# Sliding-window attention, Mish layer and experts: the activation, the weight conversion, the normalisation and the order of the blocks are rewritten

## The chip, the cores and the metric

One core of a Trainium2 chip runs the whole program. The metric is the device time of one execution in microseconds (us); the median of several executions is given. TensorE (PE, with its weight loads as PEld), VectorE (DVE), ScalarE (ACT), GpSimd (POOL) and SyncE (SP, here the issuer of DMAs) have queues of their own, each worked off in order.

## What is computed

```python
# q, k, v: (2, 8, 768, 64); window 128, 4 sinks
scores = matmul(q, k.T) / sqrt(64)
keep = (pos < n_sink) | ((rel >= 0) & (rel < window))
a = softmax(where(keep, scores, -1e9))            # sum + 1e-9
x = matmul(a, v)                                  # -> 1536 tokens x 512
h = x @ w_in                                      # 512 -> 2048, float64 weights
x = (h * tanh(softplus(h))) @ w_out               # 2048 -> 512, float64 weights
p = probs / (probs.sum(-1) + 1e-9)
out = sum(p[:, e] * (relu(x @ w1[e]) @ w2[e]) for e in range(4))   # 512 -> 1024 -> 512
```

## The kernel before, in words

**Attention.** `banded` goes over 24 items (batch, block of 256 queries, pair of heads). `attention_item` makes four score tiles of 128 queries each (two heads `j`, two halves `t`), in PSUM bank `sc`. VectorE adds the mask and takes the maximum (line 273), ScalarE the exponential with its sum (277), VectorE adds 1e-9 and takes the reciprocal (278, 279). Then the probabilities `pr` are normalised in place (286, 289): `c.turn("norm")` deals the two heads of items 0 to 15 to VectorE and GpSimd in turn, and those of items 16 to 23 to GpSimd alone. TensorE transposes them (309), ScalarE copies the result (311), TensorE multiplies with `v` (323), and `evac_x` writes the attention output as a high and a low part, `xh` (204) and `xl` (205). Blocks after the first one have four sink columns; three small VectorE copies (298 to 300) gather them as high, high and low parts, two transposes (316) and one matmul with `vsk` (328) add them.

The first `FP_ITEMS` = 16 items multiply float32 scores directly (two matmul records a tile). The last eight split `qk` into `hi` and `lo` (`attention_prep`, 239) and use three single-pass matmuls a tile.

**The first layer pair.** The hidden dimension of 2048 is cut into units 0 to 3 of 512. Each unit's float64 weights come as pairs of 32-bit words and are converted in pieces of [128, 512] by `split_double` (line 136 on ScalarE, 137 to 139 and 141 to 144 on VectorE): four operations with one tensor input, three with two. The high part goes to its tile by a DMA from `cv_h`. A unit has eight such pieces. `layer1` makes blocks `h` of 128 hidden features x up to 512 tokens with 12 matmuls, `mish` turns each into `gh` and `gl`, and `layer2` makes blocks `o` of 12 matmuls from four of these. `mish` is four ScalarE operations (571 to 574), two VectorE operations (575, 576), a square on ScalarE (578), another VectorE operation (579), and a product, a rounded copy and a difference, which from unit 1 on are all GpSimd's (583, 111, 121). For unit 0 the `Turns` lists mix the engines.

**The second layer pair.** Units 4 to 11 are the four experts in halves; ReLU on ScalarE (508), the low part on VectorE (509), the weighted sum on VectorE (558); GpSimd splits the float32 weights (111, 121).

**Order.** `stream` yields all four `h` of a chunk of tokens, then all four `o` of the chunk before. Unit 0's stream is interleaved with the attention: `banded` draws one step after each item from item `LAG` = 12 on, and two conversion pieces after each item. This sets priorities: a scheduler at compile time fixes the order of each queue, and moves later steps ahead where it expects an engine to be free. During the attention there is one PSUM bank for `h` and one for `o`; later there are four of each. `gh` and `gl` have six buffers each.

Of the kernel before, what the change touches and what calls it, by code (L numbers as in the profile page):

```python
# [18 lines left out]
C2, C1, C0 = 0.4889076793633006, -0.9463237919407588, -0.8989585617169157  # L19
TINY_HI = 3.4332275390625e-05  # L20
# [6 lines left out]
LAG = 12  # L27
FP_ITEMS = 16
WARM = 12


ENGINES = dict(
    norm=16 * "vp" + 16 * "p", sq="a", sq0=8 * "v" + 8 * "a", g="p", g0="pv", gh="p", gh0="ap", gl="p",
    gl0=8 * "p" + 8 * "v",
)


class Turns:


    def __init__(self, nc, **lists):
        engines = {"a": nc.scalar, "v": nc.vector, "p": nc.gpsimd}
        self.lists = {k: [engines[x] for x in v] for k, v in lists.items()}
        self.n = dict.fromkeys(lists, 0)

    def __call__(self, kind):
        self.n[kind] += 1
        return self.lists[kind][(self.n[kind] - 1) % len(self.lists[kind])]

# [35 lines left out]
def setup(c):  # L85
# [4 lines left out]
    ident_r = c.const.tile([P, P], F32R, name="ident_r")  # L90
    nc.vector.tensor_copy(ident_r, ident)
    c.ident_r = ident_r
    zero = c.acc[:, 2, 0:P]
    nc.gpsimd.memset(zero, 0.0)
    c.zero = zero
# [28 lines left out]
def split_double(c, pool, hi, lo, words):  # L124
# [7 lines left out]
    a = pool.tile([P, n], I32, tag="cv_a", name="cv_a")  # L132
# [23 lines left out]
def sink_values(c, a):  # L156

    nc = c.nc
    n = c.B * c.H // 2
    raw = c.acc[0:96, 4:6].rearrange("p a w -> p (a w)").rearrange("p (n d) -> p n d", n=n)  # L160
    nc.gpsimd.memset(raw, 0.0)
    for r in range(3):
        nc.sync.dma_start(out=raw[32 * r:32 * r + 2 * SINKS], in_=c.vsink)
    vsk = a.one.tile([96, n, P], F32R, name="vsk")
    nc.gpsimd.tensor_scalar(vsk, raw, 1.0, 0.0, ALU.mult, ALU.add)
    nc.gpsimd.tensor_tensor(vsk[32:64], raw[32:64], vsk[32:64].bitcast(F32), ALU.subtract)
    return vsk


def mask_parts(c):  # L170
# [11 lines left out]
    c.masks = [c.const.tile([P, P + SEG], F32, name=f"mask{i}") for i in range(3)]  # L182
# [25 lines left out]
def attention_pools(c, ctx):  # L208
    nc = c.nc
    a = Ctx()  # L210
    a.one = ctx.enter_context(c.tc.tile_pool(name="a_one", bufs=1))
# [4 lines left out]
    a.st = ctx.enter_context(c.tc.tile_pool(name="a_st", bufs=1))  # L216
# [5 lines left out]
    for t in a.sk:  # L222
        nc.vector.tensor_copy(
            t.rearrange("p n s d -> p n (s d)"), c.zero[:, 0:96].unsqueeze(1).to_broadcast([P, 2, 96])
        )
# [538 lines left out]
```

## Time and profile before

| | |
|---|---|
| median of 3 runs | 973.71 us (973.03 to 981.35) |
| the profiled execution, its own time | 972.71 us |
| its span, first to last instruction | 970.9 us |
| TensorE busy, records | 930.2 us (96%), 4292 |
| VectorE busy | 507.2 us (52%) |
| ScalarE busy | 330.6 us (34%) |
| GpSimd busy | 334.9 us (34%) |
| mean granted TensorE clock | 0.968 of full speed |

Matmuls are pipelined, so the durations of TensorE's records overlap and its busy time says little; how far apart matmuls start, and how many records fall into a stretch, says more. Shares over the whole span mix stages with different limits, so the rows further down are taken by stage.

### The profile page before, as it was taken

The numbers are of one execution on the slowest core, as the hardware profiler recorded it, in microseconds if no ns is written. First come the engines' busy times: TensorE is split into PE (matmuls) and PEld (weight loads), VectorE is DVE, ScalarE is ACT, GpSimd is POOL, SyncE is SP. The second block draws the span as 40 slices with busy tenths as digits, with TensorE's granted clock in tenths as the row PEclk, the third lists the DMA queues.
The fourth block names the chain that finished last, engine by engine and source line by source line (L and its number), as shares of the span: only waits on it lengthen the run. The fifth ranks groups of instructions, "written<-read, shape, count | busy, mean of one in ns | idle before, by whom it ended". The sixth has DMA issues, their size and how long they took to land.

```text
span 970.9 us, 11590 instructions
## 1 busy us (share of the span) xinstructions
PE 930.2 (96%) x4292; PEld 740.6 (76%) x4292; DVE 507.2 (52%) x1005; ACT 330.6 (34%) x709; POOL 334.9 (34%) x260
## 2 busy tenths in 40 slices
PE   7989989999897999999999999999999999999997
PEld 5566767887675777777888888888888888888886
DVE  6998795899999947586111223222222223222223
ACT  4577766665554446553222001011000011111000
POOL 3324573026456688895022202220221122110000
PEclk7699988999999999999999999999999999999999
DMA  7642240332322300100111011101110110000012
GB/s 235 191 152 64 74 140 24 107 122 98 120 81 94 119 22 22 44 24 22 43 44 44 2 43 43 44 1 44 44 44 0 44 44 1 1 1 0 1 44 90
DMA packets 33777, 57.65 MB, mean 59 GB/s; under 512 B 4376, under 2 KB 12824, under 8 KB 33712
## 3 DMA queue, kind: packets, MB, share of 16 engines
q1 hardware_dynamic: 33712, 56.82, 18.5%
q8 instruction: 36, 0.59, 0.2%
q14 instruction: 29, 0.24, 0.1%
HBM read 45.28 MB, written 3.15 MB: 50 GB/s over the span
## 4 chain that ended last, share of the span: by engine, by line
PE 71%; DVE 18%; POOL 5%; issue 4%; ACT 1%; DMA 1%; DVEq 0%; POOLq 0%
PE h L499 32%; PE o L550 27%; PE o L526 5%; PE sc L267 3%; PE pv L323 2%; DVE u L575 2%; PE tp L309 2%; POOL r L583 2%; DVE cv_h L139 2%; DVE cv_a L143 1%; DVE w L576 1%; DVE r L579 1%; DVE pr L273 1%; POOL gl L121 1%; DVE cv_r L142 1%
## 5 line engine op out<-in xcount | busy, mean ns | idle before, releaser
L499 PE MATMUL h<-xh,wih 128*128 128x512 f32 (+1 forms) x592 | 231.7, 391 | 12.7 <-DVE w L576 12.5
L499 PE MATMUL h<-xh,wil 128*128 128x512 f32 (+1 forms) x592 | 229.1, 387 | 0.0
L499 PE MATMUL h<-xl,wih 128*128 128x512 f32 (+1 forms) x592 | 228.6, 387 | 0.0
L508 ACT ACTIVATE gh<-h 128x512 fp32r<-128x512 f32 x96 | 57.2, 598 | 399.2 <-PE o L550 269.1
L558 DVE SCALAR_TENSOR_TENSOR acc<-o,pn,acc 128x512 f32<-128x512 f32 (+1 forms) x85 | 63.3, 745 | 228.4 <-PE o L550 228.4
L550 PE MATMUL o<-wol,gh 128*128 128x512 f32 (+1 forms) x388 | 150.1, 387 | 0.0
L550 PE MATMUL o<-woh,gh 128*128 128x512 f32 (+1 forms) x388 | 150.1, 387 | 0.0
L550 PE MATMUL o<-woh,gl 128*128 128x512 f32 (+1 forms) x388 | 149.9, 387 | 0.0
L509 DVE SCALAR_TENSOR_TENSOR gl<-h,gh 128x512 fp32r<-128x512 f32 x96 | 65.8, 691 | 154.9 <-ACT gh L508 154.9
L499 PEld LDWEIGHTS h<-xh,wih 128*128 128x128 f32 x592 | 112.2, 190 | 42.6 <-DVE w L576 17.6
L499 PEld LDWEIGHTS h<-xl,wih 128*128 128x128 f32 x592 | 112.2, 190 | 23.3 <-issue 0.9
L499 PEld LDWEIGHTS h<-xh,wil 128*128 128x128 f32 x592 | 112.2, 190 | 21.8
L583 POOL TENSOR_TENSOR r<-r,w 128x512 f32<-128x512 f32 (+1 forms) x44 | 69.2, 1572 | 89.4 <-DVE r L579 81.6
L526 PE MATMUL o<-gh,woh 128*128 128x512 f32 (+1 forms) x208 | 80.0, 386 | 7.6 <-POOL gh L111 5.2
L550 PEld LDWEIGHTS o<-woh,gh 128*128 128x128 f32 x388 | 72.9, 188 | 14.9
L550 PEld LDWEIGHTS o<-wol,gh 128*128 128x128 f32 x388 | 72.9, 188 | 14.8
L550 PEld LDWEIGHTS o<-woh,gl 128*128 128x128 f32 x388 | 72.9, 188 | 14.8
L526 PE MATMUL o<-gh,wol 128*128 128x512 f32 (+1 forms) x208 | 78.5, 378 | 0.0
L526 PE MATMUL o<-gl,woh 128*128 128x512 f32 (+1 forms) x208 | 74.8, 384 | 3.0 <-POOL gl L121 2.9
L111 POOL TENSOR_SCALAR woh<-stage 128x1024 fp32r<-128x1024 f32 x16 | 17.5, 1113 | 162.6 <-PE o L550 155.1
L111 POOL TENSOR_SCALAR wih<-stage 128x1024 fp32r<-128x1024 f32 x16 | 17.9, 1138 | 154.7 <-PE h L499 154.7
L575 DVE SCALAR_TENSOR_TENSOR u<-w,r 128x512 f32<-128x512 f32 (+1 forms) x52 | 43.9, 844 | 31.6 <-ACT r L574 31.6
(104 smaller groups left out, 1284.0 us busy)
## 6 DMA issues: line engine op xcount, KB each, us to landing
stage<-in_moe_w_dram SPq DMA_DIRECT2D x32, 512.0 KB, 3.7
stage<-in_moe_w_in_dram SPq DMA_DIRECT2D x16, 512.0 KB, 3.7
stage<-in_moe_w_out_dram SPq DMA_DIRECT2D x16, 512.0 KB, 3.7
wih<-cv_h SPq DMA_DIRECT2D x16, 256.0 KB, 2.8
woh<-cv_h SPq DMA_DIRECT2D x16, 256.0 KB, 2.3
acc<-in_v_dram SPq DMA_DIRECT2D x16, 192.0 KB, 2.6
out_dram<-acc SPq DMA_DIRECT2D x11, 256.0 KB, 2.0
qk<-in_qk_dram SPq DMA_DIRECT2D x8, 324.0 KB, 4.3
```

The costliest lines, as they stand in the source:

```text
L111: eng.tensor_scalar(out, src, 1.0, 0.0, ALU.mult, ALU.add)
L139: nc.vector.scalar_tensor_tensor(h, w_hi, -0x40000000, a, ALU.bitwise_and, ALU.bitwise_or)
L267: nc.tensor.matmul(sc, lhsT=qq[rows, t * P:(t + 1) * P], rhs=kk[rows, k0:k0 + sw], start=s == 0, stop=s == len(terms) - 1,)
L309: nc.tensor.transpose(tp[:, sg], pr[:, j, t, col:col + P], c.ident)
L499: nc.tensor.matmul(h, lhsT=wis[sw][:, k, fs], rhs=x[sx][:, k, cols], start=k == 0 and t == 0, stop=k == KT - 1 and t == 2,)
L508: nc.scalar.activation(gh, h, AF.Relu)
L509: nc.vector.scalar_tensor_tensor(gl, h, 0.0, gh.bitcast(F32), ALU.max, ALU.subtract)
L526: nc.tensor.matmul(o, lhsT=wos[sw][:, f, ds], rhs=g[f][sx], start=f == 0 and t == 0, stop=f == NF - 1 and t == 2,)
L550: nc.tensor.matmul(o, lhsT=g[f][sx][:, ds], rhs=wos[sw][:, f, ms], start=f == 0 and t == 0, stop=f == NF - 1 and t == 2,)
L558: nc.vector.scalar_tensor_tensor(y, o, pcol, y, ALU.mult, ALU.add)
L575: nc.vector.scalar_tensor_tensor(u, w, 1.0, r, ALU.add, ALU.mult)
L583: c.turn("g" + f).tensor_tensor(r, r, w, ALU.mult)
```

## The change

- `mish` becomes nine operations on fixed engines: ScalarE tanh, square, square, exp, square and the rounded copy `gh`; VectorE three operations; GpSimd the difference `gl`. The exponential's result `r` is written to PSUM (two banks), so that each VectorE operation has one operand in PSUM. `h` is read by the last of them. The sign of the sum is turned, and line 534's subtraction becomes an addition.
- To make room, `h` and `o` have three banks each instead of four. `gh` and `gl` have seven buffers instead of six.
- `split_double` takes two slices at once, [128, 1024], from loads of 1 MB; `cv_h` and `cv_r` have one buffer, `cv_a` two.
- `stream` alternates: h h o h o h o o, where `o` is of the chunk before.
- `LAG` is 5; one conversion step (of 1024) is drawn after each item.
- All items use float32 scores; the split is gone.
- All normalising, the addition of 1e-9 and the sink gather (one operation) are GpSimd's. One transpose and two 128-wide float32 matmuls add the sinks; `vsk` stays in a part of `acc`.

```diff
-LAG = 12
-FP_ITEMS = 16
+LAG = 5
...
-    a = pool.tile([P, n], I32, tag="cv_a", name="cv_a")
+    hi, lo = (x.rearrange("p k f -> p (k f)") for x in (hi, lo))
+    a = pool.tile([P, n], I32, tag="cv_a", name="cv_a", bufs=2)
...
-            terms = ((hi, hi), (lo, hi), (hi, lo)) if lo is not None else ((hi, hi),)
-            for s, (qq, kk) in enumerate(terms):
...
+            nc.tensor.matmul(sc, lhsT=raw[rows, t * P:(t + 1) * P], rhs=raw[rows, k0:k0 + sw], start=True, stop=True)
...
-    nc.vector.tensor_scalar(sm, sm, 1e-9, None, ALU.add)
+    nc.gpsimd.tensor_scalar(sm, sm, 1.0, 1e-9, ALU.mult, ALU.add)
     nc.vector.reciprocal(sm, sm)
     pts = []
+    if i > 0:
+        sk = a.sm.tile([P, 2, 2, SINKS], F32, tag="sk", name="sk")
+        nc.gpsimd.tensor_tensor(
+            sk, pr[:, :, :, P:SEG].rearrange("p h t s -> p t h s"),
+            sm.rearrange("p (h t) -> p t h", h=2).unsqueeze(3).to_broadcast([P, 2, 2, SINKS]), ALU.mult,
+        )
     for j in range(2):
-        eng = c.turn("norm")
-        if eng is nc.vector or i == 0:
+        if i == 0:
             for t in range(2):
-                o = pr[:, j, t, 0:P if i == 0 and t == 0 else full]
-                eng.tensor_scalar(o, o, sm[:, 2 * j + t:2 * j + t + 1], None, ALU.mult)
+                o = pr[:, j, t, 0:P if t == 0 else full]
+                nc.gpsimd.tensor_scalar(o, o, sm[:, 2 * j + t:2 * j + t + 1], None, ALU.mult)
         else:
             o = pr[:, j, :, 0:full]
-            eng.tensor_tensor(o, o, sm[:, 2 * j:2 * j + 2].unsqueeze(2).to_broadcast([P, 2, full]), ALU.mult)
+            nc.gpsimd.tensor_tensor(o, o, sm[:, 2 * j:2 * j + 2].unsqueeze(2).to_broadcast([P, 2, full]), ALU.mult)
...
-        for t in range(2):
-            nc.tensor.transpose(ts[:, t], sk[:, t].rearrange("p s d -> p (s d)"), c.ident_r)
+        nc.tensor.transpose(ts, sk.rearrange("p t h s -> p (t h s)"), c.ident)
...
-        nc.tensor.matmul(
-            pv, lhsT=a.vsk[:, b * (c.H // 2) + hp], rhs=st, start=False, stop=True, skip_group_check=True
-        )
+        for t in range(2):
+            nc.tensor.matmul(
+                pv[:, t * P:(t + 1) * P], lhsT=a.vsk[:, t, b * (c.H // 2) + hp], rhs=st, start=False, stop=t == 1,
+                skip_group_check=True,
+            )
...
-                for k in range(KT):
-                    split_double(c, self.cv, hi[:, k], lo[:, k], load_double(c, w, k))
+                for k in range(0, KT, 2):
+                    split_double(c, self.cv, hi[:, k:k + 2], lo[:, k:k + 2], load_double(c, w, k))
                     yield
...
-        prev = None
+        prev = iter(())
         for n, t0, cw in chunks:
             g = []
-            yield from self.layer1(n, t0, cw, g)
-            if prev:
-                yield from self.layer2(*prev)
-            prev = n, t0, cw, g
-        yield from self.layer2(*prev)
+            here = self.layer1(n, t0, cw, g)
+            for which in (here, here, prev, here, prev, here, prev, prev):
+                if next(which, run) is not run:
+                    yield
+            for which in (here, prev):
+                for _ in which:
+                    yield
+            prev = self.layer2(n, t0, cw, g)
+        yield from prev
...
-        w, r, u = (self.tp.tile([P, self.CW], F32, tag=t, name=t)[:, 0:cw] for t in ("w", "r", "u"))
+        w, u = (self.tp.tile([P, self.CW], F32, tag=t, name=t)[:, 0:cw] for t in ("w", "u"))
+        r = self.pr.tile([P, self.CW], F32, tag="r", name="r")[:, 0:cw]
         nc.scalar.activation(w, h, AF.Tanh, scale=0.5)
         nc.scalar.activation(w, w, AF.Square, scale=-0.5, bias=0.5)
-        nc.scalar.activation(r, w, AF.Square, scale=C2, bias=C1)
-        nc.scalar.activation(r, r, AF.Exp, bias=C0)
+        nc.scalar.activation(u, w, AF.Square, scale=C2, bias=C1)
+        nc.scalar.activation(r, u, AF.Exp, bias=C0)
         nc.vector.scalar_tensor_tensor(u, w, 1.0, r, ALU.add, ALU.mult)
-        nc.vector.scalar_tensor_tensor(w, w, 1.0, h, ALU.subtract, ALU.mult)
-        if c.turn("sq" + f) is nc.scalar:
-            nc.scalar.activation(u, u, AF.Square, bias=-1.5)
-            nc.vector.scalar_tensor_tensor(r, u, 0.75, r, ALU.add, ALU.mult)
-        else:
-            nc.vector.scalar_tensor_tensor(u, u, 3.0, u, ALU.subtract, ALU.mult)
-            nc.vector.scalar_tensor_tensor(r, u, 3.0, r, ALU.add, ALU.mult)
-        c.turn("g" + f).tensor_tensor(r, r, w, ALU.mult)
-        split(c, gh, gl, r, c.turn("gh" + f), c.turn("gl" + f))
+        nc.scalar.activation(u, u, AF.Square, scale=ROOT2, bias=-1.5 * ROOT2)
+        nc.vector.scalar_tensor_tensor(u, u, 1.5, r, ALU.add, ALU.mult)
+        nc.vector.scalar_tensor_tensor(w, u, 1.0, h, ALU.subtract, ALU.mult)
+        split(c, gh, gl, w, nc.scalar, nc.gpsimd)
...
-        run(w, 2)
+        run(w, 1)
...
-    x.psum(ctx, 4, 4)
+    x.psum(ctx, 3, 3, 2)
     w = x.weights(1)
-    run(w, 4)
+    run(w, 2)
```

During the attention `r` lies in SBUF (one buffer), since all eight PSUM banks are taken there.

## Rows read from the trace of the kernel before

**Rows 1.** stages: length, busy us (xinstructions) of PE, PEld, DVE, ACT, POOL; granted clock; DMA

```profile
15.00:60.00 45.00, 43.26 (x182) 25.02 (x182) 41.78 (x140) 28.95 (x90) 16.05 (x13) 0.70 0.69 225
60.00:125.00 65.00, 61.33 (x424) 44.19 (x423) 55.97 (x206) 48.68 (x158) 32.06 (x34) 1.00 0.27 78
125.00:155.00 30.00, 26.55 (x160) 18.82 (x159) 26.72 (x87) 19.28 (x60) 18.32 (x16) 0.72 0.41 126
155.00:183.00 28.00, 28.00 (x158) 22.33 (x159) 17.10 (x34) 18.32 (x35) 5.27 (x5) 1.00 0.06 21
183.00:225.00 42.00, 42.00 (x208) 35.70 (x208) 41.34 (x74) 29.31 (x54) 11.57 (x9) 1.00 0.43 138
225.00:325.00 100.00, 85.48 (x346) 67.10 (x345) 99.93 (x144) 50.66 (x84) 58.02 (x43) 0.95 0.31 100
325.00:452.00 127.00, 118.62 (x498) 92.65 (x497) 87.01 (x107) 65.75 (x111) 100.14 (x75) 0.99 0.12 38
452.00:971.00 519.00, 513.94 (x2279) 425.87 (x2277) 130.50 (x183) 65.13 (x108) 88.70 (x52) 1.00 0.09 29
```

**Rows 2.** the chain that ended last, from 452 us: start, us, what

```profile
454.43 10.88 PE h L499 x48
465.31 10.88 PE o L550 x48
```

**Rows 3.** TensorE's waits, 225 to 325 us: us in total, times, longest

```profile
PE h L499 <- DVE w L576: 9.6, 6, 3.4
```

**Rows 4.** groups by line, 225 to 325 us: shapes, count | busy us, mean ns | idle before

```profile
L583 POOL TENSOR_TENSOR r<-r,w 128x512 f32<-128x512 f32 x15 | 27.2, 1815 | 39.8 <-DVE r L579 36.0 <-PE o L526 3.7
...
L121 POOL TENSOR_TENSOR gl<-r,gh 128x512 fp32r<-128x512 f32 x14 | 21.3, 1519 | 1.1
...
L139 DVE SCALAR_TENSOR_TENSOR cv_h<-stage,cv_a 128x512 int32<-128x512 int32 x13 | 13.6, 1043 | 0.0
...
L575 DVE SCALAR_TENSOR_TENSOR u<-w,r 128x512 f32<-128x512 f32 x14 | 11.6, 825 | 0.0
...
L576 DVE SCALAR_TENSOR_TENSOR w<-w,h 128x512 f32<-128x512 f32 x14 | 9.5, 678 | 0.0
L573 ACT ACTIVATE r<-w 128x512 f32<-128x512 f32 x15 | 9.5, 631 | 11.0 <-POOL gl L121 10.8
...
L534 DVE TENSOR_TENSOR acc<-acc,o 128x512 f32<-128x512 f32 x12 | 7.7, 675 | 0.0
```

**Rows 5.** VectorE's timeline: start us, us, engine, line, operation, out<-in

```profile
245.05 0.42 DVE L142 TENSOR_SCALAR cv_r<-cv_h 128x512 int32<-128x512 int32 x1
245.38 0.68 DVE L575 SCALAR_TENSOR_TENSOR u<-w,r 128x512 f32<-128x512 f32 x1
245.99 0.68 DVE L143 SCALAR_TENSOR_TENSOR cv_a<-stage,cv_a 128x512 f32<-128x512 uint32 x1
...
254.47 1.49 DVE L142 TENSOR_SCALAR cv_r<-cv_h 128x512 int32<-128x512 int32 x1
```

**Rows 6.** GpSimd's timeline at the same time

```profile
254.23 1.45 POOL L583 TENSOR_TENSOR r<-r,w 128x512 f32<-128x512 f32 x1
```

**Rows 7.** the chain's lines, 60 to 125 us, shares of the stretch

```profile
by line: PE sc L267 13.5%; DVE pr L273 9.7%; PE tp L309 8.1%; PE h L499 7.8%; PE pv L323 7.2%; DVE pr L286 7.1%; PE o L526 6.2%; DVE sk L298 5.6%; DVE r L582 4.2%; issue 3.3%; DVE hi L115 3.1%; DVE xl L205 2.7%; DVE u L575 2.4%; DVE wol L14
```

**Rows 8.** TensorE's timeline: exact scores, then split scores

```profile
68.93 0.71 PE L267 MATMUL sc<-qk 64*128 64x260 f32 x4
69.57 1.09 PE L323 MATMUL pv<-pt,acc 128*64 128x256 f32 x12
...
129.02 0.28 PE L267 MATMUL sc<-hi,lo 64*128 64x260 f32 x1
129.14 0.28 PE L267 MATMUL sc<-lo,hi 64*128 64x260 f32 x1
```

**Rows 9.** normalising on GpSimd, lines 289 and 286: ns min/median/max, first and last start

```profile
L289 POOL TENSOR_TENSOR pr<-pr,sm x24: 1052/1055/1813, 39.1 to 156.4; 128x520 f32<-128x520 f32 x24
...
L286 POOL TENSOR_SCALAR pr<-pr,sm x16: 608/932/1430, 11.8 to 105.4; 128x128 f32<-128x128 f32 x8, 128x256 f32<-128x256 f32 x8
```

**Rows 10.** the copy of `xh`, line 204, columns as in rows 9

```profile
L204 ACT ACTIVATE xh<-pv x24: 358/378/386, 22.2 to 178.4; 128x256 fp32r<-128x256 f32 x24
```

More of the change, by code (lines that the diff above doesn't have):

```diff
@@ L159, in sink_values @@
     n = c.B * c.H // 2
[L160 to L166, printed above, removed]
+    vsk = c.acc[0:4 * SINKS, 4:8].rearrange("p a w -> p (a w)").rearrange("p (t n d) -> p t n d", t=2, n=n)
+    nc.gpsimd.memset(vsk, 0.0)
+    for t in range(2):
+        nc.sync.dma_start(out=vsk[2 * SINKS * t:2 * SINKS * (t + 1), t], in_=c.vsink)
     return vsk
@@ L181, in mask_parts @@
     nc.vector.tensor_scalar(diag, rel, 0.0, None, ALU.is_lt)
-    c.masks = [c.const.tile([P, P + SEG], F32, name=f"mask{i}") for i in range(3)]
+    c.masks = [c.const.tile([P, n], F32, name=f"mask{n}") for n in (P, 2 * P, P + SEG)]
 def banded_masks(c):
@@ L220, in attention_pools, with attention_values @@
     a.pv = ctx.enter_context(c.tc.tile_pool(name="a_pv", bufs=1, space=PSUM))
-    a.sk = [a.one.tile([P, 2, 3, 32], F32R, name=f"sk{i}") for i in range(2)]
[L222 to L225, printed above, removed]
-    a.it = 0
-    a.vsk = None
-    return a
-def attention_prep(c, a, raw, exact, b, hp, i):
-    nc = c.nc
-    n = QW + c.KW[min(i, 1)]
-    hi, lo = raw, None
-    if not exact:
-        hi = a.qk.tile([P, QW + c.KW[1]], F32R, tag="qk", name="hi")
-        lo = a.qk.tile([P, QW + c.KW[1]], F32R, tag="qk", name="lo")
-        split(c, hi[:, 0:n], lo[:, 0:n], raw[:, 0:n], nc.vector, nc.gpsimd)
+    a.vsk = sink_values(c, a)
+    return a
+def attention_values(c, a, b, hp, i):
     v = a.v.next()
     n0 = 0 if i else 1
-    nc.sync.dma_start(
+    c.nc.sync.dma_start(
         out=v[:, n0:3],
@@ L245, in attention_prep @@
     )
-    return hi, lo, v
+    return v
 def attention_item(c, a, b, hp, i, prep):
@@ L327, in attention_item @@
     if i:
-        nc.tensor.matmul(
-            pv, lhsT=a.vsk[:, b * (c.H // 2) + hp], rhs=st, start=False, stop=True, skip_group_check=True
-        )
+        for t in range(2):
+            nc.tensor.matmul(
+                pv[:, t * P:(t + 1) * P], lhsT=a.vsk[:, t, b * (c.H // 2) + hp], rhs=st, start=False, stop=t == 1,
+                skip_group_check=True,
+            )
     evac_x(c, b * c.S + i * QW, hp, pv)
@@ L413, in load_double @@
 def load_double(c, w, k):
-    raw = c.stage.next().bitcast(I32)
-    c.nc.sync.dma_start(out=raw, in_=w[k * P:(k + 1) * P, :])
+    raw = c.pairs.next().bitcast(I32)
+    c.nc.sync.dma_start(
+        out=raw.rearrange("p (k f) -> p k f", k=2), in_=w[k * P:(k + 2) * P, :].rearrange("(k p) f -> p k f", p=P)
+    )
     return raw.rearrange("p (f w) -> p f w", w=2)
@@ L675, in swa_mish_experts_kernel @@
     c.nc.scalar.preload_act_table_set("exp_and_others")
-    c.turn = Turns(nc, **ENGINES)
     c.acc = c.const.tile([P, c.T // P, c.DM], F32, name="acc")
-    c.stage = Ring([c.const.tile([P, STAGE], F32, name=f"stage{n}") for n in range(4)])
+    stage = c.const.tile([P, 4 * STAGE], F32, name="stage")
+    c.stage = Ring([stage[:, n * STAGE:(n + 1) * STAGE] for n in range(4)])
+    c.pairs = Ring([stage[:, n * STAGE:(n + 2) * STAGE] for n in (2, 0)])
     load_scalars(c)
```

62 lines of the change are left out of this document (15 added, 47 removed).

## The prediction

> **What bounds the kernel now.** I read the busy time by stage first, then the chain of work that ended last, then the waits, the groups by line and the timelines inside the stages that are not at full rate. From 452 us to the end TensorE alone sets the time: its busy column is full and VectorE is busy 130 of 519 us [rows 1]. The chain there is nothing but blocks of 48 matmuls in 10.88 us, so 0.227 us for a matmul of 512 columns [rows 2]. That is the second expert layer (units 4 to 11). The change leaves its matmuls as they are, so these 519 us stay.
>
> Ahead of it lie two stretches that can move. From 183 to 452 us unit 0 is finished and units 1 to 3 run. The matmul records of this stretch are 208 + 346 + 498 = 1052 [rows 1]. The last four output blocks of unit 0's second 256-token chunk (48 records) are 256 wide; matmuls of 260 columns start 0.12 us apart [rows 8]. At full rate the stretch would take 1004 x 0.227 + 48 x 0.12 = 233 us, and it takes 269. So **36 us** of it are TensorE waiting. From 225 to 325 us VectorE is busy 99.93 of 100 us [rows 1], and the wait that TensorE names is for the activation's `w` of line 576, which frees a score bank `h` [rows 3]. From 325 to 452 us GpSimd is busy 100 of 127 us [rows 1], and VectorE is no longer full.
>
> Why is VectorE full? One conversion piece of 512 columns is four single-input operations and three with two inputs. Undisturbed, the first kind holds its queue for 0.33 us (from 245.05 to 245.38) and the second for 0.61 (from 245.38 to 245.99) [rows 5], so a piece costs 4 x 0.33 + 3 x 0.61 = 3.15 us. From 225 to 325 us there are 14 activations of three operations, 12 accumulations and 13 pieces [rows 4]: 14 x 1.83 + 12 x 0.61 + 13 x 3.15 = 74 us. The other 26 us are operations that got longer: line 142 took 1.49 us at 254.47 where it had taken 0.42 at 245.05 [rows 5], just while GpSimd ran line 583 [rows 6]. Not every operation suffers. Line 576, with one operand in PSUM, averages 678 ns, and line 534, which reads PSUM too, 675 ns; line 575, with both in SBUF, averages 825, and line 139 averages 1043 [rows 4]. GpSimd was busy 58 us there [rows 1], so each of its microseconds cost VectorE 26/58 = 0.46 us.
>
> The Trainium skill ("SBUF — State Buffer", Who interferes with whom) says that GpSimd and VectorE share one pair of SBUF ports under an exclusive lock, taken by VectorE's fast single-input modes and by operations with two SBUF inputs, and that a VectorE operation with at most one SBUF input outside those modes is not held up. The trace agrees on all kinds: 1.49 against 0.42 us, 825 and 1043 against 678 ns.
>
> From 15 to 183 us the attention runs with unit 0 under it. TensorE's busy column is nearly full, at a granted clock of 0.70 from 15 to 60 us and 0.72 from 125 to 155 (a mixture of its two levels, 1.2 and 2.4 GHz), and VectorE is busy 41.8 of 45, 56 of 65 and 26.7 of 30 us in the first three parts [rows 1]. The chain from 60 to 125 us has more of VectorE's lines than of any single TensorE line [rows 7].
>
> **The change part by part: units 1 to 3.** The new activation has three VectorE operations, each with one operand in PSUM (`r` twice, `h` once). By line 576 each costs 0.68 us and holds its queue for 0.61; GpSimd keeps only `gl`. Per unit of 12 blocks VectorE now has 12 x (3 + 1) x 0.61 = 29 us, and four pieces of 1024 columns at no more than 2 x 3.15 = 6.3 us each, 25 us; what the wider piece saves on fixed cost I set to nothing, for want of a row. That is 54 us. GpSimd's share falls from 58 us over 14 to 15 blocks, 4.0 us each, to one operation of 1.52 us [rows 4], 18 us a unit; at 0.46 this costs VectorE 8 us, at least half of it, since over half of its time is now in operations that are not held up. VectorE comes to 58 to 62 us. TensorE needs 288 x 0.227 = 65.3 us a unit. ScalarE takes six operations of 0.63 us a block [rows 4], 45 us, and four wider absolute values of at most 1.3 us: 51 us. So TensorE becomes the bound, by 3 to 7 us a unit. In unit 3, which converts no doubles, GpSimd loses the same 2.5 us a block, and TensorE leads by more.
>
> The other side of this part is cover. The stream now goes h h o h o h o o. From the end of the fourth `h` to the first use of its `g` lie four blocks and nine matmuls, 57 x 0.227 = 12.9 us; in the old order it was eight blocks and nine, 23.8. The activation chain is 0.60 + 4 x 0.63 on ScalarE (tanh, three squares, exp), 3 x 0.68 on VectorE, 0.63 for `gh` and 1.5 for `gl`: 7.3 us. Nine handovers may thus queue for 5.6 us together before TensorE waits. An `h` bank is held 5.2 us by the same rows, and with three banks the shortest time to its next use is four blocks, 10.9 us, so three banks suffice. An activation that is late delays its `o` block, and every `h` behind that in TensorE's order. I take a quarter of the 36 us as staying (9 us, 0.13 us at each of 72 blocks), so **-27 us**; the bounds are -36 (TensorE never waits) and 0 (the queueing eats the cover).
>
> **The attention.** The chain from 60 to 125 us has 7.1 + 5.6 + 4.2 + 3.1 = 20% in VectorE lines that go: normalising (286), the sink copies (298), an activation step (582), the split (115) [rows 7]. That is 13 us. But the work comes back on GpSimd, serially: it gets the first normalisation of each of items 0 to 15, eight at 1.05 us and sixteen of line 286's at a median of 0.93 [rows 9], 23 us; and 16 sink gathers and 24 small additions, for which GpSimd has no row, between nothing and 0.61 us (the shortest of line 286 [rows 9]), so at most 24 us. It loses the eight splits and two of three steps of each activation. From 15 to 155 us it was busy 66 us of 140 [rows 1]; it goes to some 85, not full, but behind the exponentials of each item now stand a GpSimd addition, VectorE's reciprocal, the gather and two normalisations in one queue. Three `pr` buffers overlap items, which hides most of it. Of the 13 us I keep half, -6.
>
> TensorE gets more to do. Items 16 to 23 have exact scores: two tiles side by side take 0.64 us (from 68.93 to 69.57), where a tile split into three takes 3 x 0.12 [rows 8]. An item's four tiles cost 1.3 us if they pair and 2.6 if they do not, against 1.44, so eight items cost -1 to +9; I take +4, as pairs and single tiles both occur. The sinks trade two transposes and a 256-wide matmul for one transpose and two 128-wide ones in full precision: near +0.1 us for 16 items, **+2**. The smaller lag constant (5 for 12) moves no work out of the stretch: unit 0's blocks ran under the attention already [rows 1, 7], and they stay fillers with one `h` bank. Sum for the attention **0**, bounds -13 and +13. The larger loads are costed at nothing: the queue moves the same weights, and TensorE's attention work covers the first conversion. If that cover went, unit 0 would start late by one piece, 6 us.
>
> **Sum.** The profiled execution took 972.7 us, 1.8 us more than its span and 1.0 below the median of 973.7. 972.7 - 27 + 0 = **946 us**.
>
> **Rivals.** (1) *Halved cover.* ScalarE has 51 and VectorE about 60 of 65 us filled, in fixed order, so the nine handovers may queue longer than 5.6 us, and TensorE stands before `o`. Against it: the chain loses two GpSimd operations and its longest waits. If 8 of the 36 us are gained, 972.7 - 8 = 965 us.
>
> (2) *GpSimd holds up the attention.* Unit 0's conversion runs in these same 15 to 75 us and is made of just the operations that get longer under GpSimd. By 0.46 us for each of some 20 added GpSimd microseconds it loses 9 us, and with +6 for TensorE's added work and no gain from the chain the result is 972.7 - 27 + 15 = 961 us. The lock rule of the Trainium skill ("SBUF — State Buffer", Summary: rules for kernel authors) speaks for this rival: schedule the loser of the lock off the critical path, and this change puts GpSimd work on it.
>
> (3) *The slow clock spreads: slower.* From 60 to 125 and from 155 to 183 us the granted clock is 1.00, with TensorE busy 61 of 65 and 28 of 28 us; from 125 to 155, with TensorE busy 26.6 of 30, it is 0.72 [rows 1]. If the longer serial step leaves such gaps in all items, the 93 us that are now at 1.00 run at the 0.70 of the first part: 93/0.70 = 133, +40. 972.7 - 27 + 40 = 986 us. It decides from an attention longer by 27 us. Against it: more unit 0 and score work fills gaps.
>
> **How the numbers follow.** My forecast, 930 to 960 us, gets 0.61; a still better case near TensorE's bound (972.7 - 36 - 13 = 924) 0.05; rival 1 0.13, rival 2 0.10, rival 3 0.11. About 1%, 10 us, can be told from no change. Faster takes the forecast, the better case and rival 2, which falls below 964, with none of rival 1: 0.76. Same is rival 1: 0.13. Slower is rival 3: 0.11. The range goes from the lower bound of both terms, 923, to no gain at all, 974; it leaves out rival 3 and a little below.
>
> **What would show it.** Right: from the end of the attention to the second layer, 112 matmul records in 25 us nearly throughout, VectorE below 95% there, its activation lines at 0.68 us whatever GpSimd does, GpSimd below 30%, and the attention's last `xh` near the 178 us of now [rows 10]. Wrong: TensorE waiting for `gh` or `gl` at `o` in units 1 to 3 (rival 1), conversion lines of several microseconds and an attention past 190 us (rival 2), or a granted clock below 0.8 between 60 and 180 us (rival 3).

## The result, and the profile after

The changed kernel takes **965.27 us** (median of 4 executions, 962.4 to 966.62) against 973.37 us before. The ratio is 0.9898, with a 95% interval of 0.9849 to 0.9948. The interval leaves out 1, so the gain of 8 us is real; but it is no more than the 1% that the prediction called the least that can be told, and less than the 2% from which a kernel is called faster here. The forecast was 946, so 8 us came of 27. The time lies inside the range, at its slow side, and on the very figure of rival 1; whether rival 1's cause is behind it is the first thing to find out. (Executions over 1.5% longer than the fastest of their kernel, two of `narrow` and one of `lag12_rsbuf` below, count in the medians and ranges given, but not in the ratios.)

The profiled execution took 966.62 us with a span of 964.8. These are its stages; columns as in [rows 1]: length, then the busy time and instructions of PE, PEld, DVE, ACT and POOL, the granted clock, the DMA share and GB/s.

```profile
15.00:60.00 45.00, 41.42 (x150) 22.46 (x147) 33.83 (x83) 24.15 (x68) 28.28 (x28) 0.58 0.67 233
60.00:125.00 65.00, 64.45 (x430) 44.89 (x428) 37.95 (x139) 52.84 (x170) 39.86 (x57) 0.97 0.38 115
125.00:155.00 30.00, 30.00 (x193) 20.85 (x192) 13.70 (x50) 23.41 (x68) 13.00 (x20) 1.00 0.11 32
155.00:183.00 28.00, 27.53 (x159) 19.53 (x159) 7.13 (x18) 14.38 (x33) 5.03 (x6) 1.00 0.00 1
183.00:225.00 42.00, 33.64 (x144) 26.64 (x142) 30.54 (x38) 24.94 (x42) 8.82 (x5) 0.95 0.30 104
225.00:325.00 100.00, 90.13 (x368) 71.99 (x369) 88.75 (x111) 64.05 (x104) 24.61 (x16) 0.93 0.34 125
325.00:452.00 127.00, 126.98 (x561) 104.80 (x560) 71.44 (x106) 80.00 (x138) 52.69 (x36) 1.00 0.11 34
452.00:965.00 513.00, 507.80 (x2252) 420.79 (x2250) 126.66 (x177) 62.39 (x103) 85.52 (x50) 1.00 0.09 29
```

From 325 us on TensorE is at full rate: 561 records in 127 us are 0.226 us each, where there were 498 before. What is missing lies ahead of that. From 183 to 225 us there are 144 records where 42/0.227 = 185 would fit, and from 225 to 325 us 368 for 440. Together with 561 for 559 that is 111 records short, 25 us. Before, the same stretch lost 36 us. So units 1 to 3 gained 11 us instead of 27, and the attention lost some of that again: the last `xh` is written at 182.1 us, where [rows 10] have 178.4. In this line the minimum, median and maximum in ns stand ahead of the first and the last start:

```profile
L177 ACT ACTIVATE xh<-pv x24: 362/384/387, 24.3 to 182.1; 128x256 fp32r<-128x256 f32 x24
```

The groups from 225 to 325 us, as in [rows 4] (shapes, count | busy us, mean ns | idle before):

```profile
L95 POOL TENSOR_TENSOR gl<-w,gh 128x512 fp32r<-128x512 f32 x16 | 24.6, 1538 | 80.2 <-ACT gh L87 78.3 <-PE h L456 1.9
...
L114 DVE SCALAR_TENSOR_TENSOR cv_h<-stage,cv_a 128x1024 int32<-128x1024 int32 x7 | 11.0, 1572 | 0.0
L535 DVE SCALAR_TENSOR_TENSOR w<-u,h 128x512 f32<-128x512 f32 x16 | 10.9, 679 | 0.4
L532 DVE SCALAR_TENSOR_TENSOR u<-w,r 128x512 f32<-128x512 f32 x16 | 10.9, 679 | 5.0 <-ACT r L531 5.0
L534 DVE SCALAR_TENSOR_TENSOR u<-u,r 128x512 f32<-128x512 f32 x15 | 10.2, 679 | 2.3 <-ACT u L533 2.1
```

All three VectorE operations of the activation now take 679 ns. GpSimd is busy 24.6 of 100 us, where it was 58.0 in [rows 1]. TensorE's waits from 183 to 325 us (us in total, times, longest) still name the activation's last step, as [rows 3] do. All its waits there add up to 19 of the 25 us; the granted clock there is 0.95 and 0.93, where it was 1.00 and 0.95 before:

```profile
PE h L456 <- DVE w L535: 14.2, 6, 5.4
PE o L483 <- ACT gh L87: 2.0, 1, 2.0
```

Yet VectorE is no longer full all the way. It is busy 7.13 of 28 us from 155 to 183 and 2.20 of 13 from 183 to 196, and then 77 of 79 us to 275. In these 79 us TensorE has 239 records where 79/0.227 = 348 would fit, nearly all of the 111 that are missing:

```profile
196.00:225.00 29.00, 21.48 (x84) 16.72 (x84) 28.34 (x35) 19.61 (x32) 7.53 (x4) 0.93 0.44 150
225.00:250.00 25.00, 19.57 (x75) 15.07 (x75) 24.51 (x29) 15.78 (x25) 5.21 (x3) 0.88 0.50 186
250.00:275.00 25.00, 21.59 (x80) 17.05 (x80) 24.27 (x31) 14.36 (x22) 6.51 (x4) 0.86 0.41 145
275.00:300.00 25.00, 25.00 (x112) 20.71 (x111) 16.94 (x25) 17.88 (x30) 5.26 (x5) 1.00 0.11 43
```

The conversion of unit 1 keeps VectorE full there, and that conversion begins late. SyncE's DMA queue shows it: the first DMA of unit 1's high part (line 115) waits for line 534, an operation of the activation, and is issued at 195.73 us. In the kernel before, the same DMA (line 140) went out at 178.45. First a line of that queue's waits from 140 to 230 us, then its timeline, after and before:

```profile
SPq L115 <- DVE u L534: 55.0, 1, 55.0
```

```profile
195.73 4.62 SPq L115 DMA_DIRECT2D wih<-cv_h  x2
```

```profile
178.45 5.42 SPq L140 DMA_DIRECT2D wih<-cv_h  x4
```

The activation for which it waits is the fourth and last of unit 0's third chunk (512 tokens). ScalarE's timeline shows the four begin 14 to 16 us apart, the third under the attention and the fourth behind it (the last line holds two, the second of the next chunk):

```profile
146.22 0.60 ACT L528 ACTIVATE w<-h 128x512 f32<-128x512 f32 x1 [1.24 <-PE h L456]
162.19 0.60 ACT L528 ACTIVATE w<-h 128x512 f32<-128x512 f32 x1 [2.69 <-PE h L456]
176.27 0.60 ACT L528 ACTIVATE w<-h 128x512 f32<-128x512 f32 x1 [2.23 <-PE h L456]
189.81 1.09 ACT L528 ACTIVATE w<-h 128x512 f32<-128x512 f32 x2 [3.72 <-PE h L456]
```

Which edit does this? One that the prediction priced at nothing: `LAG`. Interleaved with the attention are 24 - `LAG` steps of unit 0's stream. The first chunk gives 4 steps (its `h`), the second 8 (its `h`, and the `o` of the first). So `LAG` = 12 draws 12 steps, just these two chunks. `LAG` = 5 draws 19: the third chunk's four `h` and three of the second's `o` too. The steps that are drawn there use the attention's set of PSUM banks, with one for `h`, and keep `r` in SBUF, in memory that is later unit 1's weight tile (`first.close()`, then `m_w1`).

### The profile page after: what moved, and what is told of

It is laid out like the page before. It is cut to its first block, busy times and chain, and to the rows that moved or that the text cites. A ratio compares the mean times of both kernels' runs of the same rounds, so it can differ in the third digit from the quotient of the medians.

```text
span 964.8 us, 11096 instructions
## 1 busy us (share of the span) xinstructions
PE 932.9 (97%) x4292; PEld 740.9 (77%) x4292; DVE 417.4 (43%) x754; ACT 352.1 (36%) x745; POOL 264.4 (27%) x233
## 4 chain that ended last, share of the span: by engine, by line
PE 86%; issue 5%; DVE 4%; DMA 2%; POOL 1%; ACT 0%; DVEq 0%; POOLq 0%; ACTq 0%
PE h L456 38%; PE o L507 27%; PE o L483 10%; PE sc L224 4%; PE pv L270 3%; PE tp L257 3%; PE pv L276 1%; DVE cv_h L114 1%; POOL gl L95 1%; DMA qk<-in_qk_dram 1%; DVE cv_a L118 1%; DMA stage<-in_moe_w_in_dram 1%; POOL pr L245 1%; DVE w L535 0%; DVE cv_a L112 0%
## 5 line engine op out<-in xcount | busy, mean ns | idle before, releaser
L456 PE MATMUL h<-xh,wih 128*128 128x512 f32 (+1 forms) x592 | 231.3, 391 | 14.7 <-DVE w L535 14.2
L95 POOL TENSOR_TENSOR gl<-w,gh 128x512 fp32r<-128x512 f32 (+1 forms) x52 | 69.8, 1342 | 186.9 <-ACT gh L87 184.7
L532 DVE SCALAR_TENSOR_TENSOR u<-w,r 128x512 f32<-128x512 f32 (+1 forms) x52 | 33.4, 642 | 47.1 <-ACT r L531 46.9
```

The lines of the kernel that those rows point to most:

```text
L95: eng_lo.tensor_tensor(lo, src, hi.bitcast(F32), ALU.subtract)
L456: nc.tensor.matmul(h, lhsT=wis[sw][:, k, fs], rhs=x[sx][:, k, cols], start=k == 0 and t == 0, stop=k == KT - 1 and t == 2,)
L532: nc.vector.scalar_tensor_tensor(u, w, 1.0, r, ALU.add, ALU.mult)
```

## Experiments

**How they are compared.** The times of one kernel differ by up to 17.6 us between executions (`narrow`), and they follow the mean granted clock of the execution. Over 95 executions of all kernels, straight lines with one common slope and a height of its own for each kernel have -673 us per 1.0 of clock, that is 6.7 us less for each 0.01 more, with 1.2 us left over. Beside each median stands what that line gives at a clock of 0.970: "at 0.970". Before: 973.1. After: 964.0. This takes it that a kernel doesn't change its own clock; where one does, by waiting less, the figure takes that part of its gain away, so the medians stand beside it.

**The lag alone, in both kernels.** Theory: the smaller lag costs the gain. Rivals: the order of the blocks, or the wider pieces.

```diff
-LAG = 5      # the changed kernel: lag12
+LAG = 12
```

> The changed kernel with the lag constant back at 12, nothing else. Theory A (late start): the changed kernel's seven extra blocks go one by one through the attention's single h bank, and the attention's memory, which unit 1's weight tiles reuse, comes free only after the last of them: the first DMA into unit 1's high part left at 195.7 us against 178.5 before, with VectorE idle until then and full from 196 to 275. It expects that DMA near 180 us and a time of 950 to 956 us, 9 to 15 below the changed kernel's 965. Theory B (the conversion of 1024 columns with one cv_h and cv_r buffer is too slow) and theory C (the alternating order leaves too little cover) expect no move beyond 3 us.

947.24 us (942.53 to 947.5), ratio 0.9698 [0.9648, 0.9747]; 949.0 at 0.970. **15 us of one constant** (18 by the medians), and the forecast's 946 is met, by a kernel with one constant changed back. 9 to 15 us had been expected. The span is 19.4 us shorter than after. It can be counted in TensorE's records. Here are the three stages from 155 us on; those after have 159, 144 and 368:

```profile
155.00:183.00 28.00, 28.00 (x176) 22.50 (x175) 17.00 (x23) 19.70 (x39) 5.27 (x4) 1.00 0.12 40
183.00:225.00 42.00, 37.49 (x161) 29.39 (x160) 39.89 (x50) 27.71 (x47) 10.64 (x4) 1.00 0.51 186
225.00:325.00 100.00, 95.36 (x413) 78.14 (x412) 81.14 (x108) 70.51 (x118) 27.52 (x20) 0.98 0.25 90
```

17 + 17 + 45 records more, and 7 more ahead of 155 us: 86 x 0.227 = 19.5 us. (For each of the 15 variants of the changed kernel this count from 15 to 325 us gives the difference of the spans within 1.3 us, so the stretch up to 325 us holds the whole effect.) The four activations of the third chunk now follow each other 3 to 6 us apart and start before the attention's end (172.7 us):

```profile
154.31 0.60 ACT L528 ACTIVATE w<-h 128x512 f32<-128x512 f32 x1 [0.96 <-PE h L456]
159.74 0.60 ACT L528 ACTIVATE w<-h 128x512 f32<-128x512 f32 x1 [0.42 <-PE h L456]
163.07 0.60 ACT L528 ACTIVATE w<-h 128x512 f32<-128x512 f32 x1 [0.24 <-POOL gl L95]
168.94 0.57 ACT L528 ACTIVATE w<-h 128x512 f32<-128x512 f32 x1
```

The DMA goes out at 172.20 us and VectorE converts at once (17.00 us busy from 155 to 183, not 7.13):

```profile
172.20 5.05 SPq L115 DMA_DIRECT2D wih<-cv_h  x2
```

And behind the attention TensorE finds `o` blocks of the second chunk ready, as the chain shows:

```profile
176.00 4.57 PE o L483 x38
```

In the changed kernel there are 12 such records, from 184.02 to 185.32 us.

```diff
-LAG = 12     # the kernel before: old_lag5
+LAG = 5
```

> The kernel before with the lag constant at 5, nothing else. Theory A expects a later first DMA into unit 1's high part (190 us or more against 178.5) and a time 5 to 15 us above the 973.4 of before. Theories B and C expect no move beyond 3 us.

981.42 us (979.23 to 982.8), ratio 1.0058 [1.0008, 1.0107]; 977.5 at 0.970. The lag costs there too, but 4 us at equal clock, not 15, and the DMA leaves at 181.75 us, only 3 later than before: the theory had expected 190 or more. In this kernel the third chunk's four activations start at 127.05, 144.23, 167.27 and 176.68 us, so the fourth still falls under the attention (last `xh` at 181.8). They too lie 9 to 23 us apart, but the chunk starts 19 us earlier than in the changed kernel; why it does was not tested. TensorE is busy 25.61 us from 155 to 183 (28.00 before) at a clock of 0.79 (1.00 before).

**How much lag.**

```diff
-LAG = 5      # lag9 and lag14
+LAG = 9      # 14 in lag14
```

> The changed kernel with lag 9: 15 blocks are drawn under the attention, so two activations of the third chunk go through the attention's single h bank, where lag 5 sends all four and lag 12 none. If the time goes with the number of 512-wide activations in that bank (theory A2): between the 965 of lag 5 and the 947 of lag 12, 952 to 960 us, the attention's last xh between 173 and 182 us, and the third and fourth activation of the third chunk close together. If only a fourth activation behind the attention's end matters: at the level of lag 12, 944 to 950.

> The changed kernel with lag 14: ten blocks, so that the second chunk's last two output blocks of the first are drawn later and no 512-wide activation lies in the single bank, as with lag 12. Theory A2 expects the level of lag 12, within 4 us of 947. If instead every later step helps by what it takes out of the attention: 940 to 944.

`lag9`: 950.09 us (940.93 to 951.74), ratio 0.9735 [0.9676, 0.9793]; 949.7 at 0.970, no different from 12. It draws 15 steps, two `h` of the third chunk among them. The second and third activation start together at 167.92 us, the fourth at 177.97, and the DMA leaves at 174.49, ahead of the last `xh` (175.1):

```profile
167.92 1.09 ACT L528 ACTIVATE w<-h 128x512 f32<-128x512 f32 x2 [2.15 <-PE h L456]
177.97 0.57 ACT L528 ACTIVATE w<-h 128x512 f32<-128x512 f32 x1
```

So two activations of the third chunk in the single bank cost nothing that can be told, against the expectation that the time goes with their number. The 15 us come between a lag of 9 and one of 5: with the last four steps, two `h` and two `o`, or with the earlier place of all of them, which no run tells apart.

`lag14`: 954.67 us (950.9 to 957.64), ratio 0.9814 [0.9769, 0.986]; 954.5 at 0.970. Its DMA is the earliest of all, at 165.16 us, but TensorE is busy 21.63 of 28 us from 155 to 183 and makes 149 records there. Both expectations (within 4 us of 947, or 940 to 944) are missed: it is 5.5 us above `lag12` at equal clock. Its last `xh` comes at 165.7 us, so the attention is shorter with fewer steps in it, and TensorE is the emptier behind it. Too few steps cost something as well; too many cost more.

**Is it the memory of `r`?** If the late DMA is the whole cause, freeing it brings the gain back at `LAG` = 5. `r_last` opens the block's PSUM set, and with it the SBUF buffer of `r`, behind the attention's pools; `r_own` gives the buffer memory of its own (and one `gh`/`gl` buffer less to make room, which `gp6` does alone).

```diff
     first = ExitStack()
-    x.psum(first, 1, 1)          # r_last: one line down
     a = attention_pools(c, first)
+    x.psum(first, 1, 1)
...
-        self.gp = ctx.enter_context(tp(name="m_g", bufs=7))
+        self.gp = ctx.enter_context(tp(name="m_g", bufs=6))      # r_own, gp6
+        self.r1 = ctx.enter_context(tp(name="m_r1", bufs=1))     # r_own
...
+        self.pr = (PSUM pool) if nr else self.r1                 # r_own
```

> The changed kernel, lag constant 5, with two lines swapped: the attention's own tiles are placed first and its SBUF buffer for r (and its h and o banks) behind them. The weight tiles of unit 1 are placed over this memory in the order high part of wi, low part, high and low part of wo; so far the buffer r lies under the first of them. Theory A1 (the high part waits for the last read of r in that buffer, the third chunk's fourth activation): the first DMA into unit 1's high part leaves within 3 us of the attention's last xh, 13 us earlier than in the changed kernel, and the time falls by 5 to 12 us, to 953 to 960. Theory A2 (the single h bank delays the blocks themselves, memory is not the point): that DMA may leave early, the time stays within 4 us of 965.

`r_last`: 961.8 us (957.4 to 963.94), ratio 0.9852 [0.9801, 0.9903]; 960.9 at 0.970. It doesn't test what it was made for: the DMA still waits for line 534 (50.8 us) and leaves at 189.47.

> The changed kernel, lag 5, with six buffers each of gh and gl: the partner of the next two runs. With lag 12 six buffers took 942.8 us where seven took 947.2, so within 5 us of 965 is expected by every theory.

`gp6`: 965.85 us (958.57 to 966.22), ratio 0.9885 [0.9819, 0.995]; 963.3 at 0.970. The buffer costs nothing.

> The run before it, but the buffer of r that unit 0 uses under the attention lies in memory of its own for the whole run, no longer in the attention's memory (swapping the order of the two, in an earlier run, left the DMA into unit 1's high part waiting for line 534 as before). Theory A1 (unit 1's conversion waits for the memory under r): the first such DMA leaves within 3 us of the attention's last xh instead of 13 us after it, and the time falls by 5 to 12 us against its partner. Theory A2 (what costs is that the third chunk's four activations and the blocks behind them go one by one through a single h bank, at 10 to 16 us each): the DMA leaves early and the time stays within 4 us of the partner.

`r_own`: 962.89 us (955.81 to 966.5), ratio 0.9868 [0.9795, 0.9941]; 961.3 at 0.970, so **2 us of the 15**. The wait is gone and the DMA leaves at 180.73 us, ahead of the last `xh` (181.3), yet the 5 to 12 us that the memory theory expected do not come. Its stages show what that moved (lines of this kernel are one higher):

```profile
183.00:225.00 42.00, 28.35 (x120) 22.16 (x118) 37.82 (x47) 22.68 (x39) 5.98 (x4) 0.89 0.46 164
225.00:325.00 100.00, 96.54 (x406) 78.48 (x406) 81.86 (x107) 67.91 (x113) 26.27 (x17) 0.96 0.28 102
```

From 225 to 325 us there are 406 records, 38 more than after (8.6 us) and nearly those of `lag12` (413). But from 183 to 225 there are 24 fewer than after, and 41 fewer than in `lag12`. TensorE stands still there for one `gh`, in its waits from 183 to 325 us:

```profile
PE o L484 <- ACT gh L87: 7.7, 1, 7.7
```

It is the `gh` of the fourth activation. Its three VectorE steps stand among conversion steps and end at 199.37 us. Its copy stands behind the absolute value of the next conversion piece in ScalarE's queue, and that waits for its load, which holds the copy up for another 2.0 us:

```profile
198.69 0.68 DVE L536 SCALAR_TENSOR_TENSOR w<-u,h 128x512 f32<-128x512 f32 x1
```

```profile
200.35 1.12 ACT L111 ACTIVATE cv_a<-stage 128x1024 f32<-128x1024 f32 x1 [3.99 <-DMA stage<-in_moe_w_in_dram]
201.36 0.63 ACT L87 ACTIVATE gh<-w 128x512 fp32r<-128x512 f32 x1
```

In this kernel the fourth activation starts at 190.14 us and the second chunk's `o` blocks are used up, so nothing covers that wait. So the early DMA by itself gives back 2 us: what TensorE gains later it loses behind the attention, where it has nothing ready while the last activation is still on its way. That the ready blocks are the rest of the 15 us is read from these traces and not tested by itself.

**Is it the one bank?** Two `h` banks under the attention, at the price of one of its three score banks.

```diff
-    a.ps = ctx.enter_context(c.tc.tile_pool(name="a_ps", bufs=3, space=PSUM))
+    a.ps = ctx.enter_context(c.tc.tile_pool(name="a_ps", bufs=2, space=PSUM))
...
-    x.psum(first, 1, 1)
+    x.psum(first, 2, 1)
```

> The changed kernel, lag 5, with two h banks under the attention and two banks for scores instead of one and three. Theory A2: the third chunk's activations come at half the distance (now 146, 162, 176 and 190 us), the fourth before the attention's end, and the time falls by 6 to 12 us, to 953 to 959, less what the scores lose by one bank. Theory A1 expects the same early DMA and so the same sign: r_own tells them apart. If the scores need their third bank more: slower than 965.

`h2`: 963.0 us (962.28 to 965.9), ratio 0.9886 [0.983, 0.9943]; 966.2 at 0.970. The four activations now start at 145.91, 146.41, 165.53 and 170.00 us, all under the attention, and from 225 to 325 us it makes 400 records. But the last `xh` comes at 192.3 us, 10 later than after, and the time doesn't fall, where 953 to 959 had been expected. All eight banks are taken, so the `h` bank without the price of a score bank stays untested.

**The order of the blocks** (rival 1), at both lags and with 6 and 7 buffers for `gh` and `gl`.

```diff
-            here = self.layer1(n, t0, cw, g)
-            for which in (here, here, prev, here, prev, here, prev, prev):
...
+            yield from self.layer1(n, t0, cw, g)
+            yield from prev
```

> The changed kernel with the old order of blocks (four h, then four o of the chunk before), with seven gh and gl buffers and three banks each of h and o. Theory C expects 955 to 960 us, 5 to 10 below the changed kernel. Theory A expects a late first DMA still (four h of the third chunk go through the single bank) and a time within 3 us of 965, or up to 6 above, as three h banks are one too few for four h in a row. Theory B expects no move beyond 3 us.

> The changed kernel with lag 12 and the old order of blocks. With lag 5 the old order took 960.8 against 965.3 us, at a granted clock that was higher in part. If the halved cover costs (rival 1 of the prediction): 3 to 8 us below the 947.2 of lag 12. If not: within 3 us, or slower, as four h in a row find three banks.

> The changed kernel with lag 12 and six buffers each of gh and gl instead of seven: the partner of the next run, which needs the memory. If the seventh buffer matters little: within 4 us of the 947 of lag 12. If the fourth g of a chunk really has to wait for a buffer until two blocks later, as the halved cover would make it felt: 952 or more.

> The changed kernel with lag 12, six g buffers and the old order of blocks, the order of which took 941.6 us with seven buffers. If order and buffers each brought their few microseconds: 936 to 939. If what they showed was only the granted clock of those executions: 940 to 947, on the same line of time against clock as lag 12.

`old_order`: 960.79 us (955.34 to 963.9), ratio 0.9842 [0.9784, 0.99]; 962.2 at 0.970 against 964.0. `lag12_oldorder`: 941.63 us (938.25 to 949.98), ratio 0.9658 [0.9606, 0.971]; 948.1 against 949.0 of `lag12`. `lag12_gp6`: 942.79 us (938.33 to 945.48), ratio 0.9655 [0.9605, 0.9706]; 947.4. `lag12_gp6_old`: 947.42 us (946.83 to 948.56), ratio 0.9743 [0.971, 0.9775]; 947.4. The order is worth less than 2 us either way, and so is the seventh buffer. All four of lag 12 beat both kernels given; no difference among them stands at equal clock.

**The width of the pieces.** Pieces of 512 from loads of 512 KB as before, with two buffers of each `cv` tile.

```diff
-                for k in range(0, KT, 2):
-                    split_double(c, self.cv, hi[:, k:k + 2], lo[:, k:k + 2], load_double(c, w, k))
+                for k in range(KT):
+                    split_double(c, self.cv, hi[:, k:k + 1], lo[:, k:k + 1], load_double(c, w, k))
...
-        run(w, 1)
+        run(w, 2)
```

> The changed kernel with conversion pieces of 512 columns, loads of 512 KB, and two buffers each of cv_a, cv_r and cv_h, as before. Theory B expects 953 to 958 us, 7 to 12 below the changed kernel, with the stretch from 196 to 275 us near full rate. Theory A expects the DMA into unit 1's high part still near 195 us and the time within 3 us of 965; theory C too.

> The changed kernel with lag 12, six g buffers, and conversion pieces of 512 columns with two buffers of each scratch tile. With lag 12 and six buffers the time was 942.8 us, of which 183 to 325 us still hold some 10 us of waiting while units 1 and 2 are converted. If the single cv_h and cv_r of the wide pieces cause that waiting: 934 to 940 us. If the port lock and the amount of conversion do: within 3 us of 943, or up to 4 above, as narrow pieces have more fixed cost.

`narrow`, at lag 5: 962.54 us (948.12 to 965.69), ratio 0.9778 [0.9686, 0.9869]; 959.6 at 0.970, from two executions only, 4 us below after. `lag12_gp6_narrow`: 949.82 us (946.06 to 951.91), ratio 0.9756 [0.9714, 0.9798]; 949.7, 2 us above `lag12_gp6`. Small, and of either sign: at lag 12 the single `cv` buffers are not what is left.

**The parts of the gain**, at lag 12: the exponential's `r` back to SBUF (its two PSUM banks then stay empty), and items 0 to 15 with one head normalised on VectorE again.

```diff
-        self.pr = ctx.enter_context(tp(name="m_pr", bufs=nr or 1, **(dict(space=PSUM) if nr else {})))
+        self.pr = ctx.enter_context(tp(name="m_pr", bufs=1 + (nh > 1)))     # lag12_rsbuf, with gp6
...
+        eng = nc.vector if j == 0 and a.it < 16 else nc.gpsimd              # lag12_norm
```

> The same as the run before it (lag 12, six g buffers), but the exponential's result r lies in SBUF (two buffers) in all units, so that two of the three VectorE operations of an activation have two SBUF inputs. The prediction's account (operations with an operand in PSUM are not held up by GpSimd) expects lines 532 and 534 at 0.80 to 0.90 us on average against 0.68, that is 12 x 2 x 0.15 = 4 us of VectorE a unit, and 3 to 10 us more time. If PSUM operands bring nothing here, because GpSimd has so little left to do: within 2 us.

> The changed kernel with lag 12, where items 0 to 15 have the first head normalised on VectorE as before, the rest as in the change. The prediction kept 6 us of gain for the attention's VectorE lines that go and named a GpSimd that holds up the attention as a rival. If GpSimd's serial normalising costs the attention: 3 to 8 us less than lag 12, with the last xh earlier. If moving it pays: 3 to 8 us more. If it hides either way: within 2 us.

`lag12_rsbuf`: 953.06 us (946.78 to 961.39), ratio 0.9743 [0.9674, 0.9811]; 954.1 at 0.970, **7 us above** `lag12_gp6`. The lines from 183 to 440 us, first of `lag12_gp6`, then of `lag12_rsbuf`:

```profile
L532 DVE SCALAR_TENSOR_TENSOR u<-w,r 128x512 f32<-128x512 f32 x40 | 27.3, 682 | 25.8 <-ACT r L531 25.6
L534 DVE SCALAR_TENSOR_TENSOR u<-u,r 128x512 f32<-128x512 f32 x40 | 27.3, 682 | 11.4 <-ACT u L533 10.8
L535 DVE SCALAR_TENSOR_TENSOR w<-u,h 128x512 f32<-128x512 f32 x40 | 27.3, 682 | 2.3
```

```profile
L532 DVE SCALAR_TENSOR_TENSOR u<-w,r 128x512 f32<-128x512 f32 x39 | 39.0, 1001 | 33.4 <-ACT r L531 33.4
L534 DVE SCALAR_TENSOR_TENSOR u<-u,r 128x512 f32<-128x512 f32 x40 | 33.5, 840 | 12.7 <-ACT u L533 12.2
L535 DVE SCALAR_TENSOR_TENSOR w<-u,h 128x512 f32<-128x512 f32 x40 | 27.2, 681 | 2.1
```

The same operations on the same engine, one operand moved from PSUM to SBUF: 1001 and 840 ns for 682, while line 535, which reads `h` in PSUM in both kernels, is at 682 and 681. It goes with GpSimd's work: in `lag12_rsbuf` line 532 takes 1273 ns on average where a GpSimd instruction runs at the same time (21 of its operations) and 618 elsewhere (20); in `lag12_gp6` 684 and 678.

`lag12_norm`: 949.48 us (947.47 to 950.88), ratio 0.9724 [0.9682, 0.9765]; 950.2 at 0.970 against 949.0. Normalising on GpSimd gains 1 us or nothing.

## Why the prediction was wrong in one term and right in others, step by step

- **From 452 us to the end: right.** 2252 records in 513 us after, 2279 in 519 before. Nothing moved there.
- **Units 1 to 3: right as a mechanism, and right in size once the lag is back at 12.** "TensorE becomes the bound" holds nearly throughout from 275 us on in the changed kernel (112 records in 25 us from 275 to 300, 105 in the next 25, 561 in the 127 us from 325). With `LAG` = 12 the stretch from 183 to 452 us has 161 + 413 + 562 = 1136 records of 1185, so 11 us are lost, where "a quarter of the 36" was to stay. The operand in PSUM is worth 7 of the 25 us so gained. The rest (fewer GpSimd operations among it) was not taken apart. One slip in the working changes nothing: 26/58 is 0.45, not 0.46.
- **"Three banks suffice": mis-sized.** An `h` bank was to be held 5.2 us. From the start of the tanh to the end of line 535 it is a median of 10.6 us in the changed kernel for the activations from 183 to 325 us and 7.0 at lag 12, and TensorE's waits there name line 535 (14.2 and 6.9 us). Whether a fourth bank would end them was not tried, not even in `lag12_rsbuf`, which has two banks free.
- **The attention: sum 0, right once the lag is back at 12; its single terms stay open.** With lag 12 the span falls by 25.5 us and units 1 to 3 give 25 of it. Whether the -6, +4 and +2 are each right was not tested, so the 0 may hold by luck. The GpSimd terms without a row were small: 24 additions at a median of 0.193 us and 16 gathers at 0.216, 8 us in place of the bound of 24. GpSimd was busy 81 us of 140 from 15 to 155 us, 85 had been expected. In the changed kernel the last `xh` was 3.7 us late, at lag 12 it was 5.7 early.
- **The step that failed: "The smaller lag constant (5 for 12) moves no work out of the stretch", priced at nothing.** It was weighed by the amount of work only, as a change of fillers under a TensorE that is busy anyway. In the changed kernel it costs 15 us at equal clock, 18 by the medians (4 in the kernel before). It is not the amount of work that counts but which steps fall to the attention's set of banks and buffers, as the traces have it. Seven more steps are drawn there. They make the third chunk's activations pass through one `h` bank, 14 to 16 us apart; they hold memory that unit 1's weights need (DMA at 195.73 us for 172.20); and they use up the `o` blocks that would cover the stretch behind the attention. With three of the seven (`lag9`) the time is still that of lag 12. The step count, 24 - 12 = 4 + 8, stood in the code before any trace.
- **"The larger loads are costed at nothing": near enough.** The width is worth 2 to 4 us of either sign. The ground that was given, that the attention covers the first conversion, was not tested. A late start of a conversion, which the text priced at 6 us for unit 0, did come, but at unit 1 and by the lag.
- **Rival 1, 965 us: its figure, not its cause.** TensorE did stand before `o` and `h`, but mostly before 275 us, and the old order with its longer cover gains under 2 us. It falls. **Rival 2** falls too: the attention's last `xh` came at 182 us, not past 190, and normalising on VectorE again gains nothing. **Rival 3** didn't come: the clock is 0.97 and 1.00 between 60 and 180 us. From 15 to 60 us it was 0.58, but `gp6`, which has one buffer less of `gh` and of `gl`, shows 0.73 there at the same mean clock of 0.965.

**What stays open.** How the 13 us that `r_own` leaves divide between the one bank and the missing ready blocks: `h2` pays for its bank with another. Why the same lag costs the kernel before only 4 us. Giving unit 1's weights memory of their own wasn't tried. And at lag 12 some 11 us are still lost from 183 to 325 us, at line 535 (6.9 us of waits); neither the order, the width, nor the buffers of `gh` and `gl` take them away.

## What to carry to other kernels

A constant that says how early fillers are drawn also says which buffers and banks they use: count the steps that it lets in, and ask what memory they hold and what is left ready behind the stage. An operation on two inputs that slows beside another engine may be helped by one operand in PSUM, and this can be read beforehand from lines of the same kernel that have one. When a large edit brings less than its sum, undo its smallest constants first.

## What the runs showed of the hardware

**The time follows the granted clock, and that differs between executions of one kernel.** The mean clock of an execution lay between 0.956 and 0.988, that of `lag12_oldorder` alone between 0.969 and 0.983, and 0.01 of it is 6.7 us. Only one execution of each kernel has a profile, so where inside an execution the difference arises is seen only between kernels. Here is the stage from 15 to 60 us in `lag12_gp6_narrow` (mean clock 0.970) and in `narrow` (0.988), which differ in the lag and in one buffer of `gh` and `gl`:

```profile
15.00:60.00 45.00, 43.09 (x128) 21.93 (x126) 29.23 (x92) 22.32 (x69) 22.65 (x28) 0.50 0.57 194
```

```profile
15.00:60.00 45.00, 41.30 (x212) 23.69 (x212) 42.01 (x128) 34.01 (x107) 30.57 (x37) 0.88 0.72 244
```

128 records at 0.50 and 212 at 0.88: over 45 of some 947 us this is about the whole difference of the two means. A clock of 0.50 is the lower of TensorE's two levels throughout (1.2 of 2.4 GHz). What decides it wasn't found. Two medians that differ by 5 us here say little until their clocks are laid beside them: `lag12_oldorder` and `lag12` are 5.6 us apart by medians and 0.9 at equal clock.

**The lock between GpSimd and VectorE can be avoided by place.** The Trainium skill ("SBUF — State Buffer", Who interferes with whom) says that a VectorE operation with at most one SBUF input, outside the fast single-input modes, is not held up by GpSimd. `lag12_rsbuf` is the trial of it, and its trace agrees: 1001 against 682 ns, long only beside GpSimd's instructions, and 7 us of the whole.

**A queue in order passes a wait on.** In `r_own` a ScalarE operation that waited 3.99 us for a load held up a finished activation's copy behind it for 2.0 us, out of the 7.7 that TensorE waited for that copy.
